# The product with v in four column tiles of 32, and a priority of its own for every group of the plan

## The chip, the cores and the metric

The kernel runs on one NeuronCore of a Trainium2 chip. The metric is the device time of one execution, in microseconds (us). The core has five engines that work beside each other: PE (TensorE, the matrix array, whose weight loads are shown apart as PEld), DVE (VectorE), ACT (ScalarE), POOL (GpSimd) and SP (SyncE, which here only issues DMAs). Every engine takes its own instructions strictly in the order in which they are written, and waits on semaphores for the others.

## What is computed

Attention with a hash mask for 4 batches of 8 heads (768 positions, 64 numbers per head), and behind it a gated MLP:

```python
q_bits = (np.einsum('bhsd,dk->bhsk', q, proj) > 0); k_bits = ...   # 6 bits, a bucket of each row
mask = q_bucket[:, :, :, None] == k_bucket[:, :, None, :]
scores = np.where(mask, scale * np.matmul(q, k.transpose(0, 1, 3, 2)), -1e9)
scores = scores - np.max(scores, axis=-1, keepdims=True)
attn = np.exp(scores); attn = attn / (np.sum(attn, axis=-1, keepdims=True) + 1e-09)
x = np.matmul(attn, v)                     # heads side by side: 768 x 512 per batch
h = gelu(x @ w_in); u, v = halves of h; v_n = layernorm(v) * g_ln
out = x + (u * (w_sg @ v_n + b_sg)) @ w_out
```

## The kernel before

The attention works on 16 pairs of heads (4 batches, 4 pairs each). The two heads of a pair (j = 0, 1) lie side by side: 64 rows of the array for each in the scores, 64 columns for each in the product with v. The queries of a pair are done in two halves of 384. The work on PE comes in groups, each named here by its line:

- transposes (L548): q or k of the pair two ahead, six matmuls of 128x128 over the full array
- projection (L580): the hash bits of q and k of the pair two ahead, four matmuls in four column tiles of 32, fp32, 384 columns
- maxima (L626): scores of one block of 128 queries against half of the keys, four matmuls in two 64-row tiles. DVE takes the row maximum out of PSUM (L631)
- spread (L644): the maxima of half a pair turned into a row, three matmuls over the full array; ACT copies it into the features (L650)
- weights (L666): the scores again, transposed and shifted by the maximum, eight matmuls in two 64-row tiles for one block of 128 keys; ACT makes the exponential p (L671), and POOL adds the p of a half up (L680)
- product (L696): p times v for half a pair, over the six blocks of keys (kt) and the two heads: twelve matmuls, fp32, each with v as weights and 385 columns of p moving. Every fp32 matmul is two pairs of weight load and matmul in the trace, so a product is 24 matmuls there. ACT copies the result out (L711)
- sum (L720): the row sums of the half before, four matmuls in four column tiles of 32, fp32, 192 columns. From there a chain of small DMAs on SP leads (L737 sum out to memory, L738 back as `sq`) to a reciprocal on DVE (L739), two more DMAs (L741, L743) and the scaling on DVE (L745)

The hash bits take a way of their own: projection, then a compare on DVE (L583, the sign), then four DMAs on SP (L611) that put the bits beside the features `fq` and `fk`, which the maxima of that pair read. The low parts of q and k are made on DVE (L557). Preparing w_in and w_out fills DVE, POOL and ACT in between (L398 to L411).

PSUM has eight banks. A maxima or weights group and a block of transposes take two of them, a product, sum, projection or spread one. A bank pair is free again when DVE or ACT has read it.

Nothing of this order is left to a scheduler on the chip. The class `Plan` collects groups (`add`, with engine, cost, priority, form of the array, and buffers), and `order` simulates them by its own costs: at each step it takes the engine that is free first and, of the groups that are ready there, the one with the smallest priority number. The order that it finds is what each engine then executes. A priority is `2 * g` (g counts steps of a pair: six each) plus an offset by kind, plus an entry of the table `SHAPE` that is repeated with a fixed period. `TURN_PE` is the planner's cost of a change of the array's form ("row" for 64-row tiles, "col" for two tiles of 64 columns, "col32" for four of 32).

The MLP (L884 to L1130) follows for the four batches: v half of the hidden layer (L892), u half (L923 for the first batch, L1031 for the others), gate (L1097) and output projection (L1126), all over the full array.

Of the kernel before, what the change touches and what calls it, by code (L numbers as in the profile page):

```python
# [56 lines left out]
SHAPE = {"A": [-0.98, -2.55, -0.98, -3.44, -0.98, -5.54, -0.98, -3.31, -0.98, -0.98, -4.35, -0.98, -2.56, -0.98, -0.98, -0.98, -0.98, -3.67, -0.98, -0.98], "AV": [0.04, 0.0], "C": [3.53, 5.01, 6.13, 6.3], "E": [-0.97, -1.77, -2.62, -1.21, 0.19, -0.97, -1.6, 1.54, -0.61, 3.21, -2.11, -0.97], "M": [0.0, 0.0, 0.0, 0.0, -0.75, -0.2, 0.0, 0.0, 0.0, -0.91, -0.03, -1.94], "R": [2.1, 0.6, 3.9, 0.6, -0.6, 0.6, 0.6, 0.44, 0.6, 1.18, -2.15, 0.6], "S": [1.85, 0.9], "T": [0.55, 0.68], "W": [0.0, 0.0, 0.0, 0.0, 0.0, 0.0, 0.0, 0.0, 0.0, 0.0, 0.0, 0.0], "hi": [3.01, -3.43], "lo": [-0.31, -1.87], "m": [5.85, -3.2], "rc": [-3.79, 1.95], "sm": [2.31, 3.12], "un": [4.14, 8.61], "xt": [6.41, 0.14], "F": [1.92], "sg": [-6.6], "x": [1.49, 1.82]}  # L57


class Plan:  # L60


# [44 lines left out]
    def add(self, engine, cost, prio, fn, r=(), w=(), dma=0, port=None, form=None, lat=0.0, tag=None):  # L107

        port = engine == "POOL" if port is None else port
        if tag in SHAPE:  # L110
            i = self.count[tag] = self.count.get(tag, -1) + 1
            prio += SHAPE[tag][i % len(SHAPE[tag])]
        if engine == "DVE" and port:
            cost += 0.04
        g = {"e": engine, "c": cost, "p": prio, "fn": fn, "dma": dma, "n": len(self.groups), "slots": [], "port": port, "form": form, "lat": lat, "tag": tag}
        deps, after = set(), set()
        for kind, xs in (("r", r), ("w", w)):
            for x in xs:
                b, key = x if isinstance(x, tuple) else (x, None)
                if b.slots is not None and engine != "MEM":  # L120
                    g["slots"].append(b)
                if b.first is None:
                    b.first = g["n"]
                    last, gone = b.prev
                    if b.need is not None:
                        deps.add(b.need.uses[0][0])
                    if gone is not None:
                        gone.gone = True
                        deps.update(n for n, _, _ in gone.uses)
                    if last is not None and last.first != g["n"]:  # L130
                        after.add(last.first)
                elif b.first != g["n"]:
                    after.add(b.first)
                assert b.gone is False
                for n, k2, kind2 in b.uses:
                    if n != g["n"] and (kind == "w" or kind2 == "w") and (key is None or k2 is None or key == k2):
                        deps.add(n)
                b.uses.append((g["n"], key, kind))
        g["deps"], g["after"] = deps, after - deps
        self.groups.append(g)  # L140
# [138 lines left out]
def kernel(  # L279
# [16 lines left out]
    nc = tc.nc  # L296

    B, H, S, D = q.shape
    P = 128
    NT = S // P  # L300
    HT = NT // 2
    SH = S // 2
# [11 lines left out]
    Q = 32  # L314
# [99 lines left out]
    PE, DVE, ACT, POOL, SP = "PE", "DVE", "ACT", "POOL", "SP"  # L414
    xs = [dram.tile([DM, S], F32, name=f"xs_{b}") for b in range(B)]

    plan = Plan()
# [61 lines left out]
    if True:  # L479
# [9 lines left out]
        def ps_one():  # L489
            ps_s.list.append(plan.slot(ps_slots, 1, lambda i: psb[:, i, :]))  # L490
            return ps_s.list[-1]
# [26 lines left out]
        def row(j):  # L518
            return slice(j * D, (j + 1) * D)
# [167 lines left out]
        def weighted(st, hf, prio, owed, nxt=None):  # L687

            av, p, v_ = ps_one(), st.p, st.v
            half = Pair()  # L690
            half.n, half.b, half.hp, half.hf, half.av, half.sum = st.n, st.b, st.hp, hf, av, st.sum

            def product():
                for kt in range(NT):
                    for j in range(2):
                        nc.tensor.matmul(av()[row(j), :SH + 1], v_()[:, j, kt, :], p[kt]()[:, j, :], start=(kt == 0), stop=(kt == NT - 1))  # L696

            if owed is None:
                plan.add(PE, 1.3 * HT, prio, product, p + [v_], [av], form="col")
            else:  # L700
                sums, tp = owed.sum, ps_one()

                def sumup():
                    total(sums, tp)
                    if nxt:
                        nxt.project()

                plan.add(PE, 0.35 + (0.66 if nxt else 0.0), prio - 0.02, sumup, p[-1:] + [sums] + (nxt.raw if nxt else []), [tp] + ([nxt.fp] if nxt else []), form="col32")
                plan.add(PE, 1.3 * HT, prio - 0.01, product, p + [v_], [av], form="col", tag="AV")
            half.un = un = late.ring([P, SH + 1], F32, "un", 3)  # L710
            plan.add(ACT, 0.48, prio - 1, lambda: nc.scalar.copy(un(), av()[:, :SH + 1]), [av], [un], tag="un")  # L711
            if owed is not None:
                finish(owed, tp, prio)
            return half

        def total(sums, tp):
            for j in range(2):
                for a in range(2):
                    r = 64 * j + 32 * a
                    nc.tensor.matmul(tp()[r:r + 32, :QH2], ones, sums()[:, j, a * QH2:(a + 1) * QH2], start=True, stop=True)  # L720
# [77 lines left out]
        for n in range(NPAIR):  # L798
            for c in range(NT):
                if c == 0 and n + 2 < NPAIR:  # L800
                    prepare(n + 2, 2 * (g_ := NT * n) + PREP)
                hf, k0, g = c // HT, 2 * (c % HT), NT * n + c
                maxima(g + AHEAD)
                weigh(sts[n], hf, k0, 2 * g)
                if c % HT == HT - 1:
                    nxt = sts.get(n + 2) if hf else None
                    if nxt:
                        features(nxt, 0, True)
                    owed = weighted(sts[n], hf, 2 * g + AVP + OA[hf], owed, nxt)
                    if nxt:  # L810
                        rest(nxt, 2 * g + FEAT)
                if c == 1 and GPLACE <= n < GPLACE + NT:
                    t = n - GPLACE
                    for h in range(P // Q):
                        c0 = t * P + h * Q
                        dma(2 * g + 20, 0.6, cost=0.85, fn=lambda eng, t=t, h=h, c0=c0: eng.dma_start(
                            wgd[t][h * Q:(h + 1) * Q].rearrange("b (f a) -> b f a", a=Q),
                            w_sg[:, c0:c0 + Q].rearrange("(f b) a -> b f a", b=Q)), r=[ticks[-1]], w=[(wgdb, (t, h))])
                while conv and WFROM + RATE * conv[0][0] <= 2 * g:
                    at_, job, args = conv.pop(0)  # L820
                    job(plan, w_tile, *args, 2 * g + WP, after=[ticks[-1]])
# [313 lines left out]
    h = hidden_v(xx, HID)  # L1135
# [8 lines left out]
    for b in range(B):  # L1144
        p = 500 + 1000 * b
        if b:
            h = hidden_v(xx, p)
# [44 lines left out]
```

## Time and profile before

| what | value |
|---|---|
| median of 3 runs | 720.42 us (720.03 to 720.46) |
| span of the profiled execution | 719.5 us |
| PE busy | 709.6 us, 99% of the span |
| DVE, ACT, POOL busy | 566.4, 400.2 and 485.7 us (79%, 56%, 68%) |
| TensorE clock granted | full (1.000) through the span |

The span runs from the first to the last instruction of the profiled execution; the timed runs are about 0.9 us longer than it. The stages can be read off the lines on PE: up to 30.8 us the start, then the regular attention with one product in each half pair up to about 422 us, then the MLP. Since matmuls overlap in the trace (an instruction lasts longer than the distance to the next), the busy share says little about PE's pace; the distances between starts do.

### The profile page before, as it was taken

The page shows a single profiled execution, that of the slowest core. Times are in us where ns is not written, and L with a number is a line of the kernel's source. Part 1 is how long each engine was busy: PE and PEld are TensorE (multiplying, and loading weights), DVE is VectorE, ACT ScalarE, POOL GpSimd, SP SyncE. Part 2 cuts the span into 40 slices and gives each one's busy share as a digit, 9 for nine tenths or more (in the row PEclk, how much of TensorE's full clock was granted, in tenths as well). Part 3 has the DMA queues.
Part 4 walks back from the last instruction along what each step waited for, and adds up shares of the span by engine and source line. Part 5 has one row for each costly group of instructions (what it writes and reads, how often), then busy time and mean ns, then how long its engine had stood idle before and what let it go on. Part 6 is the DMA issues. An engine that isn't in the chain of part 4 may idle for free.

```text
span 719.5 us, 14177 instructions
## 1 busy us (share of the span) xinstructions
PE 709.6 (99%) x5258; PEld 558.0 (78%) x5258; DVE 566.4 (79%) x830; ACT 400.2 (56%) x645; POOL 485.7 (68%) x322
## 2 busy tenths in 40 slices
PE   8999999999999999999999999999999999999997
PEld 4676776766767676676767669997899889988996
DVE  6987789788988887888889449686698498839963
ACT  2676666657657657665765547522575265425630
POOL 4678788787877867587677848475884847484340
PEclk9999999999999999999999999999999999999999
DMA  6333643663665456256442225915531542244004
GB/s 131 86 62 95 153 112 92 138 134 105 139 131 128 106 120 141 55 139 155 107 123 57 75 86 147 230 34 142 115 96 41 137 88 89 66 111 88 1 1 117
DMA packets 181028, 75.08 MB, mean 104 GB/s; under 512 B 157920, under 2 KB 171232, under 8 KB 180960
## 3 DMA queue, kind: packets, MB, share of 16 engines
q1 hardware_dynamic: 179728, 73.33, 41.9%
q10 hardware_dynamic: 1232, 0.86, 0.4%
q8 instruction: 41, 0.67, 0.4%
q14 instruction: 27, 0.22, 0.1%
HBM read 56.33 MB, written 17.24 MB: 102 GB/s over the span
## 4 chain that ended last, share of the span: by engine, by line
PE 88%; DVE 7%; issue 2%; DMA 2%; ACT 1%; SPq 0%; DVEq 0%; ACTq 0%
PE psb L666 18%; PE psb L696 16%; PE psb L1097 13%; PE psb L892 9%; PE psb L626 8%; PE psb L1126 7%; PE psb L1031 6%; PE psb L548 3%; DVE mx L631 3%; PE psb L923 2%; PE psb L720 2%; PE psb L580 1%; PE psb L644 1%; DMA sq<-s 1%; DVE u L947 1%
## 5 line engine op out<-in xcount | busy, mean ns | idle before, releaser
L680 POOL TENSOR_TENSOR sum<-sum,p 128x768 f32<-128x768 f32 x128 | 224.4, 1753 | 82.5 <-ACT p L671 74.7
L631 DVE TENSOR_REDUCE mx<-psb 128x2 f32<-128x768 f32 x192 | 175.8, 950 | 39.5 <-PE psb L626 37.5
L671 ACT ACTIVATE p<-psb 128x768 f32<-128x768 f32 x192 | 148.9, 814 | 30.7 <-PE psb L666 22.5
L696 PE MATMUL psb<-p,v 128*64 128x385 f32 x768 | 131.2, 491 | 0.0
L696 PEld LDWEIGHTS psb<-p,v 128*64 128x64 f32 x768 | 52.3, 137 | 71.7 <-issue 62.7
L666 PE MATMUL psb<-hq,hk 64*128 64x384 f32 x384 | 72.0, 371 | 1.3 <-ACT p L671 0.7
L680 POOL TENSOR_TENSOR sum<-p,p 128x768 f32<-128x768 f32 x32 | 60.5, 1892 | 11.7 <-ACT p L671 11.5
L626 PE MATMUL psb<-fk,fq 64*128 64x384 f32 x384 | 66.6, 343 | 1.6 <-DVE mx L631 1.0
L1108 POOL TENSOR_TENSOR gs<-gt,gs 128x384 fp32r<-128x384 f32 x32 | 37.6, 1189 | 41.6 <-ACT gs L1105 38.5
L626 PE MATMUL psb<-hk,hq 64*128 64x384 f32 x384 | 64.8, 334 | 0.0
L666 PE MATMUL psb<-hq,lk 64*128 64x384 f32 x384 | 64.7, 333 | 0.0
L666 PE MATMUL psb<-lq,hk 64*128 64x384 f32 x384 | 64.6, 333 | 0.0
L666 PE MATMUL psb<-fq,fk 64*128 64x384 f32 x384 | 64.6, 333 | 0.0
L1097 PE MATMUL psb<-wgh,zh 128*128 128x384 f32 x192 | 64.3, 335 | 0.0
L1097 PE MATMUL psb<-wgh,zl 128*128 128x384 f32 x192 | 64.2, 334 | 0.0
L1097 PE MATMUL psb<-wgl,zh 128*128 128x384 f32 x192 | 64.2, 334 | 0.0
L711 ACT COPY un<-psb 128x385 f32<-128x385 f32 x32 | 15.4, 481 | 84.4 <-PE psb L696 84.4
L1126 PE MATMUL psb<-woh,gs 128*128 128x512 f32 x192 | 60.3, 391 | 0.2 <-DVE gt L1100 0.2
L908 POOL TENSOR_TENSOR zl<-y,zh 128x512 fp32r<-128x512 f32 x24 | 33.0, 1374 | 29.6 <-ACT zh L907 26.1
L666 PEld LDWEIGHTS psb<-hq,hk 64*128 64x128 f32 x384 | 36.0, 184 | 13.0 <-DVE mx L631 5.2
L1126 PEld LDWEIGHTS psb<-woh,gs 128*128 128x128 f32 x192 | 36.1, 188 | 8.2 <-DVE gt L1100 0.6
L626 PEld LDWEIGHTS psb<-fk,fq 64*128 64x128 f32 x384 | 36.0, 184 | 7.1 <-DVE mx L631 3.8
(157 smaller groups left out, 1584.8 us busy)
## 6 DMA issues: line engine op xcount, KB each, us to landing
q<-in_q_dram SPq DMA_DIRECT2D x32, 192.0 KB, 4.2
v<-in_v_dram SPq DMA_DIRECT2D x16, 384.0 KB, 3.9
rs<-r SPq DMA_DIRECT2D x64, 96.0 KB, 3.1
xs<-xt SPq DMA_DIRECT2D x32, 192.0 KB, 4.0
xl<-xs SPq DMA_DIRECT2D x16, 384.0 KB, 4.5
rx<-xs SPq DMA_DIRECT2D x96, 64.0 KB, 2.4
out_dram<-ob SPq DMA_DIRECT2D x24, 256.0 KB, 2.3
k<-in_k_dram SPq DMA_DIRECT2D x31, 192.0 KB, 4.4
```

Source lines behind the costliest of these rows:

```text
L626: nc.tensor.matmul(sc[kh]()[:, j, :SH], x[0]()[row(j), qs], x[1]()[row(j), kh * SH:(kh + 1) * SH], start=(n == 0), stop=(n == 1))
L631: plan.add(DVE, 0.95, prio + OM[2 * t + kh], lambda kh=kh: nc.vector.tensor_reduce(mx()[:, i, :, kh], sc[kh]()[:, :, :SH], axis=AX.X, op=A ...
L666: nc.tensor.matmul(sc[i]()[:, j, :SH], x()[row(j), ks], y()[row(j), cs], start=(n == 0), stop=(n == 3))
L671: plan.add(ACT, 0.81, prio, lambda i=i: nc.scalar.activation(p[i]()[:, :, :SH], sc[i]()[:, :, :SH], AF.Exp), [sc[i]], [p[i], ticks[-1]], t ...
L680: plan.add(POOL, 1.88, prio + 0.6, lambda i=i, first=first: nc.gpsimd.tensor_add(sums(), (first or sums)()[:, :, :SH], p[i]()[:, :, :SH]), ...
L696: nc.tensor.matmul(av()[row(j), :SH + 1], v_()[:, j, kt, :], p[kt]()[:, j, :], start=(kt == 0), stop=(kt == NT - 1))
L892: nc.tensor.matmul(ps(), x()[:, ts_], w[:, c, FH:FF], start=(c == 0 and n == 0), stop=(c == NC - 1 and n == 2))
L908: plan.add(POOL, 1.35, p0, lambda y=y, t=t: nc.gpsimd.tensor_sub(zl()[:, t, :], y(), zh()[:, t, :].bitcast(F32)), [y, (zh, t)], [(zl, t)])
L1031: nc.tensor.matmul(ps()[:, :SH], a()[:, c, fs], y[c](), start=(c == 0 and n == 0), stop=(c == HC - 1 and n == 2))
L1097: nc.tensor.matmul(vp()[:, :SH], z()[:, t, fs], w()[:, t, cs], start=(t == 0 and n == 0), stop=(t == NT - 1 and n == 2))
L1108: nc.gpsimd if e == POOL else nc.vector).tensor_sub(gl()[:, cs], gt(), gh()[:, cs].bitcast(F32)),
L1126: nc.tensor.matmul(po(), a()[:, ts_], w()[:, f, :], start=(f == 0 and n == 0), stop=(f == NF - 1 and n == 2))
```

## The change

Two things are edited. In `weighted`, each of the twelve matmuls of a product is split into two of 32 columns (h = 0, 1), so that four column tiles of 32 take the place of two of 64, and the product's form for the planner is "col32", as that of the sum and the projection. The planner's cost of a product stays at 1.3 * HT. And in `add`, the priority is multiplied by 100 and gets an entry of a new table, `NUDGE`, with one number for each group of the program.

```diff
+NUDGE = [
+    1272, 1955, 1479, -864, 685, 1078, 574, 133, 509, -876, 844, -2893, -188, -3059, 859, -337, ...
+    ...
@@ class Plan, add
             cost += 0.04
+        prio = round(100 * prio) + NUDGE[len(self.groups)]
@@ weighted
             def product():
                 for kt in range(NT):
                     for j in range(2):
-                        nc.tensor.matmul(av()[row(j), :SH + 1], v_()[:, j, kt, :], p[kt]()[:, j, :], start=(kt == 0), stop=(kt == NT - 1))
+                        for h in range(2):
+                            r, d = j * D + h * Q, slice(h * Q, (h + 1) * Q)
+                            nc.tensor.matmul(av()[r:r + Q, :SH + 1], v_()[:, j, kt, d], p[kt]()[:, j, :], start=(kt == 0), stop=(kt == NT - 1))

             if owed is None:
-                plan.add(PE, 1.3 * HT, prio, product, p + [v_], [av], form="col")
+                plan.add(PE, 1.3 * HT, prio, product, p + [v_], [av], form="col32")
...
-                plan.add(PE, 1.3 * HT, prio - 0.01, product, p + [v_], [av], form="col", tag="AV")
+                plan.add(PE, 1.3 * HT, prio - 0.01, product, p + [v_], [av], form="col32", tag="AV")
```

Lines of the changed kernel stand 86 higher up to the product and 88 higher behind it: L626 becomes L712, L666 L752, L644 L730, L580 L666, L583 L669, L639 L725, L739 L827, L745 L833, L696 L784 and L720 L808.

The first place is PE around the seventh product (`p` and `v` are its inputs). Before, the sum stands ahead of the product and the spread behind it:

```order
L626 MATMUL psb<-hk_2_1266,hq_2_1290 128x384 x2
L720 MATMUL psb<-sum_1132,ones 32x192 x4
L696 MATMUL psb<-p_161,v_1008 64x385 x2
L696 MATMUL psb<-p_162,v_1008 64x385 x2
L696 MATMUL psb<-p_163,v_1008 64x385 x2
L696 MATMUL psb<-p_164,v_1008 64x385 x2
L696 MATMUL psb<-p_157,v_1008 64x385 x2
L696 MATMUL psb<-p_158,v_1008 64x385 x2
L644 MATMUL psb<-identr,mst 66x128 x3
L666 MATMUL psb<-hq_1_982,hk_1_959 128x384 x2
```

In the changed kernel the same product and what follows it read:

```order
L712 MATMUL psb<-hk_2_1298,hq_2_1340 128x384 x2
L784 MATMUL psb<-p_161,v_1055 32x385 x4
L784 MATMUL psb<-p_162,v_1055 32x385 x4
L784 MATMUL psb<-p_163,v_1055 32x385 x4
L784 MATMUL psb<-p_164,v_1055 32x385 x4
L784 MATMUL psb<-p_157,v_1055 32x385 x4
L784 MATMUL psb<-p_158,v_1055 32x385 x4
L808 MATMUL psb<-sum_1175,ones 32x192 x4
L712 MATMUL psb<-fk_174,fq_173 128x384 x2
L712 MATMUL psb<-hk_2_1298,hq_2_1340 128x384 x2
L752 MATMUL psb<-hq_1_1025,hk_1_993 128x384 x2
```

The product has four tiles per block, the sum has moved behind it, and the spread has left this place: it stands twelve rows behind the sum, between a weights and a maxima group.

The second place is PE behind the eighth product, some 8 us later (`fk`, `fq`, `hk`, `hq` in one group are maxima, `hq`, `lk`, `lq` with L666 are weights). Before, four weights groups in a row are followed by three maxima groups, and a weights group:

```order
L666 MATMUL psb<-fq_173,fk_174 128x384 x2
L626 MATMUL psb<-fk_176,fq_175 128x384 x2
L626 MATMUL psb<-hk_2_1576,hq_2_1597 128x384 x2
L626 MATMUL psb<-fk_176,fq_175 128x384 x2
L626 MATMUL psb<-hk_2_1576,hq_2_1597 128x384 x2
L626 MATMUL psb<-fk_176,fq_175 128x384 x2
L626 MATMUL psb<-hk_2_1576,hq_2_1597 128x384 x2
L666 MATMUL psb<-hq_2_1290,hk_2_1266 128x384 x2
```

In the changed kernel, two weights groups behind the same product:

```order
L752 MATMUL psb<-fq_173,fk_174 128x384 x2
L712 MATMUL psb<-fk_176,fq_175 128x384 x2
L712 MATMUL psb<-hk_2_1683,hq_2_1690 128x384 x2
L752 MATMUL psb<-hq_2_1340,hk_2_1298 128x384 x2
L752 MATMUL psb<-hq_2_1340,lk_2_1375 128x384 x2
L752 MATMUL psb<-lq_2_1353,hk_2_1298 128x384 x2
L752 MATMUL psb<-fq_173,fk_174 128x384 x2
L712 MATMUL psb<-fk_176,fq_175 128x384 x2
L712 MATMUL psb<-hk_2_1683,hq_2_1690 128x384 x2
L712 MATMUL psb<-fk_176,fq_175 128x384 x2
L712 MATMUL psb<-hk_2_1683,hq_2_1690 128x384 x2
L752 MATMUL psb<-hq_2_1340,hk_2_1298 128x384 x2
```

One and then two maxima groups stand between weights groups, not three.

The third place is DVE around the sign (L583, `fc`) that belongs to the projection ahead of the eighth product. Before, the reciprocal (`sq`) stands four rows ahead of it, with a scaling (`xt`) and a maximum between:

```order
L739 RECIPROCAL sq_1479<-sq_1479 128x6
L745 SCALAR_TENSOR_TENSOR xt_1558<-un_1139,rs_1460 128x384
L631 TENSOR_REDUCE mx_99<-psb 128x2
L639 TENSOR_REDUCE mst<-mx_99 128x3x2
L583 TENSOR_SCALAR fc_1591<-psb,fcol 128x384
```

In the changed kernel:

```order
L833 SCALAR_TENSOR_TENSOR xt_1640<-un_1187,rs_1537 128x384
L717 TENSOR_REDUCE mx_99<-psb 128x2
L725 TENSOR_REDUCE mst<-mx_99 128x3x2
L827 RECIPROCAL sq_1584<-sq_1584 128x6
L669 TENSOR_SCALAR fc_1685<-psb,fcol 128x384
```

The reciprocal now stands directly ahead of the sign.

## Rows read from the trace of the kernel before

**Rows 1.** The page: span, and PE's busy time, share of span, instructions.

```profile
span 719.5 us, 14177 instructions
PE 709.6 (99%) x5258; PEld 558.0 (78%) x5258; DVE 566.4 (79%) x830; ACT 400.2 (56%) x645; POOL 485.7 (68%) x322
```

**Rows 2.** Stretches: us, busy of PE, PEld, DVE, ACT, POOL, then PEclk.

```profile
30.80:415.00 384.20, 382.07 (x3524) 269.13 (x3522) 322.41 (x392) 243.15 (x376) 296.38 (x170) 1.00 0.47 112
415.00:719.50 304.50, 299.93 (x1544) 270.24 (x1540) 220.15 (x381) 141.59 (x249) 175.40 (x130) 1.00 0.37 94
```

**Rows 3.** Timeline of PE: start us, us, engine, line, instruction, shape, count.

```profile
94.38 0.49 PE L580 MATMUL psb<-q,pw 128*32 128x384 f32 x2
...
94.71 0.49 PE L580 MATMUL psb<-q,pw 128*32 128x384 f32 x2
...
95.14 4.10 PE L696 MATMUL psb<-p,v 128*64 128x385 f32 x24
99.17 0.40 PE L644 MATMUL psb<-identr,mst 128*66 128x128 f32 x3
99.50 0.44 PE L666 MATMUL psb<-hq,hk 64*128 64x384 f32 x2
99.78 0.34 PE L666 MATMUL psb<-hq,lk 64*128 64x384 f32 x2
99.95 0.34 PE L666 MATMUL psb<-lq,hk 64*128 64x384 f32 x2
```

**Rows 4.** Timeline of weight loads (PEld), the same stretch.

```profile
94.38 0.12 PEld L580 LDWEIGHTS psb<-q,pw 128*32 128x32 f32 x2
...
95.14 0.20 PEld L696 LDWEIGHTS psb<-p,v 128*64 128x64 f32 x4 [0.62 <-ACT p L671]
95.52 0.14 PEld L696 LDWEIGHTS psb<-p,v 128*64 128x64 f32 x2 [0.18 <-issue]
95.84 0.14 PEld L696 LDWEIGHTS psb<-p,v 128*64 128x64 f32 x2 [0.18 <-issue]
```

**Rows 5.** Timeline of PE where no projection stands between sum and product.

```profile
106.17 0.53 PE L720 MATMUL psb<-sum,ones 128*32 128x192 f32 x8
106.63 4.10 PE L696 MATMUL psb<-p,v 128*64 128x385 f32 x24
```

**Rows 6.** The chain that ended last, in time: start us, us, what.

```profile
30.82 4.03 PE psb L696 x24
...
56.47 4.03 PE psb L696 x24
...
70.11 4.03 PE psb L696 x24
...
81.56 4.03 PE psb L696 x24
...
387.52 4.03 PE psb L696 x24
```

**Rows 7.** Timeline behind the eighth product: DVE's maxima and the weight load that waits.

```profile
128.85 2.69 DVE L631 TENSOR_REDUCE mx<-psb 128x2 f32<-128x768 f32 x3 [2.97 <-PE psb L626]
...
129.86 0.19 PEld L666 LDWEIGHTS psb<-hq,hk 64*128 64x128 f32 x2 [0.74 <-DVE mx L631]
```

**Rows 8.** Timeline of the start: PE's transposes, and the load that waits.

```profile
6.15 0.87 PE L548 MATMUL psb<-ident,q 128*128 128x128 f32 x6
...
7.03 0.64 PEld L548 LDWEIGHTS psb<-ident,k 128*128 128x128 f32 x6 [0.25 <-DMA k<-in_k_dram]
```

**Rows 9.** Timeline: a sign on DVE, its DMAs on SP, PE's first maxima behind.

```profile
95.34 0.68 DVE L583 TENSOR_SCALAR fc<-psb,fcol 128x384 f32<-128x384 f32 x1
...
97.24 1.22 SPq L611 DMA_DIRECT2D fk<-fc  x2
...
101.00 0.34 PE L626 MATMUL psb<-fk,fq 64*128 64x384 f32 x2
```

**Rows 10.** Waits (us in total, times, longest), and line 611's DMAs from issue to landing.

```profile
DVE sq L739 <- DMA sq<-s: 17.9, 12, 4.7
...
DMA to landing us min/median/max: 1.9/2.0/3.7
```

82 rows, old and new, of the table NUDGE are left out of this document.

## The prediction

> **What bounds the kernel.** I read the page first: PE is busy 99% of the span [rows 1], and the stretches say the same of the attention, 382.1 of 384.2 us at the full clock [rows 2]. So no other engine can be worth more than PE's own pauses, and those are mostly not idle time but badly spaced matmuls. For that I read PE's timeline by distances between starts [rows 3]. Inside weights groups a pair of matmuls starts every 0.17 us (99.78 to 99.95). Around a change of the array's form the distances grow: the last round of the projection takes 0.43 us until the product begins (94.71 to 95.14), where its first round took 0.33 (94.38 to 94.71); the product's first round takes 0.38 us and the next 0.32 (95.14, 95.52, 95.84, [rows 4]). Between product and maxima stands a third form, the spread. Then I read the chain for the pace of a half pair [rows 6]: 13.64 us with transposes and projection (56.47 to 70.11), 11.45 without (70.11 to 81.56). From the first product at 30.82 to the one at 387.52 there are 28 halves in 356.7 us; fourteen such pairs of 25.1 us would be 351.4, so about 5 us in this stretch are stalls. One of them is shown [rows 7]: three maxima groups stand together, DVE needs 2.69 us for the three, and the weights group behind them waits 0.74 us, some 0.6 more than PE's usual distance. In the MLP PE is idle 4.6 us of 304.5 [rows 2], most of it behind its last matmul.
>
> **Four tiles instead of two.** The moving columns do not change: 385 for each tile. The projection is the same form as the new product, fp32 in four column tiles of 32, and its round of four takes 0.33 us for 384 columns [rows 3]; the product's round of two tiles of 64 takes 0.32 [rows 4]. Both have 12 rounds per product, so the product's own 3.9 us stay. What could make it dearer are the loads: 48 instead of 24. The projection's load of 32 columns lasts 0.11 us (a pair of them 0.12, [rows 4]) and lies beside the matmuls before it. If the eight loads of one block of keys lay bare one after the other, 8 * 0.11 = 0.9 us would stand where two rounds take 0.65, and 32 products of six blocks would cost 32 * 6 * 0.23 = 44 us more. If they hide as in the projection it is 0, and nothing in the rows suggests less than 0. I take 0, from the row of the same form.
>
> The turn into the product goes. It costs 0.43 - 0.33 = 0.10 us on leaving the projection and 0.38 - 0.32 = 0.06 in the first round [rows 3, 4]; ahead of a product without a projection the sum leaves after 0.46 us (106.17 to 106.63, [rows 5]) where its two rounds of 192 columns, half of the projection's each, would take 0.33; that is 0.13 with the sum's own entry in it. 31 products of 32 follow a sum or a projection before: 31 * 0.16 = 5.0 us saved.
>
> **What the new order adds on PE.** I counted the turns of form in both orders from the first product to the last weights group: 153 before, 142 after. So 31 go and 20 of other kinds come. The new ones are in the places shown ahead of this: the sum moves behind the product or between two maxima groups, and the spread leaves its cheap place behind the product (where PE had to turn anyway) for one between weights and maxima. The product then turns straight into 64-row tiles 15 times more, the spread stands between two groups of 64-row tiles 5 times, a sum or product follows a spread 7 times. Their prices: leaving the product 99.17 - 95.14 = 4.03 against 12 rounds of 0.323 and the entry of 0.06, about 0.10; the first round of 64-row tiles 99.78 - 99.50 = 0.28 against 0.17, that is 0.11 [rows 3]. A turn is then between 0.10 (leaving alone) and 0.21 (both), and 20 of them 2.0 to 4.2 us. By kinds (15 at 0.21, 5 at 0.18, 7 at 0.09, less the spread's 12 turns that went, at 0.18, plus five small ones) I get 3.6 and take it. Turns together: -5.0 + 3.6 = **-1.4 us**, between -3.0 and -0.8.
>
> **What it does to the stalls.** For every tile that PE writes again I compared, in both orders, the PE work in between with the DVE or ACT work it has to wait for, at 0.9 us for a maximum [rows 7] and 0.35 for its four matmuls. Between first product and MLP seven places fall short before, by 0.2 to 0.5 us, 2.6 together; the other half of the 5 us comes from DVE's preparation of weights and from late DMAs, which an order does not show. After, two places fall short, by 0.2 and 0.3: groups of three maxima are followed by a product or by transposes, not by a weights group, as at the second place shown. So -2.1 us from what the order shows. The bounds are -5 (no stall left) and +5 (as many new ones from DVE's other work as there were before); I take -2.1, since the rest has no reason to move.
>
> **The start.** Before, q's transposes begin at 6.15 us and k's wait for their DMA until 7.03 [rows 8]. After, k's stand first, while k's second half is still the DMA issued last of the four: 7.03 - 6.15 = 0.9 us later for all that hangs on it. Against that, from there to the first product DVE sets the pace, and by the same count the new order waits about 0.5 us less there. I take +0.4, between -0.5 and +0.9.
>
> **The MLP.** Its turns are none, and in the changed order pieces of the next batch's v half stand among the output projection's matmuls. What PE can win is under 1 us [rows 2], what a late DVE addition could cost is about as much. I take 0.
>
> The sum: 719.5 - 1.4 - 2.1 + 0.4 = 716.4 us of span. The runs shown lie 0.9 above the span (720.4 against 719.5), so **717.3 us**, 0.4% faster. A difference under 0.2%, 1.4 us, can hardly be told from none here.
>
> **The rivals.** First, **the gain is eaten**: DVE is busy 322 us of 384 in the attention [rows 2], and the new order scatters its work without a period; if it makes as many stalls as it removes (0 instead of -2.1), with the start at its worst (+0.9) and the turns at -0.8, the time is 720.4 - 0.8 + 0.9 = 720.5, no change. For it: each stall of before had another reason. Against: the places that fall short went from seven to two.
>
> Second, **slower by the sign**. DVE takes its rows in order. In five of the fourteen pairs the reciprocal now stands directly ahead of the sign (the third place), so a late `sq` holds the sign, its four DMAs, and the first maxima of the next pair but one. Before, the sign began at 95.34, its last two DMAs were issued from 97.24 to 98.46, and the maxima that read them began at 101.00 [rows 9]; the last is issued at about 97.85 and lands 2.0 us later at the median of this line [rows 10], so 1.1 us is to spare, and less than nothing at the longest flight of 3.7. The reciprocal's waits are 17.9 us in 12 times, 1.5 each and 4.7 at most [rows 10]. A wait of 1.5 at the sign costs PE some 0.4, one of 4.7 some 3.6; from one of the long kind on the gain of 3.1 is gone: 717.3 + 3.6 = 720.9 with one, 724.5 with two. Against: a `sq` on an undisturbed queue has been there long before.
>
> Third, **the four tiles do not hide their loads**: 717.3 + 44 = 761 at the full price above, 739 at half of it. The projection speaks against it, but only with two rounds in a row where a product has twelve. The Trainium skill, TensorEngine Tiling (Array Packing), section Instruction Overhead, says that each matmul has about 60 cycles of overhead on trn2 and that a tiling factor should not be taken from a dimension that is already small, which speaks against this split; 768 more matmuls at 60 cycles of 2.4 GHz would be an estimated 19 us by that page. The projection's rounds of four, with the same distance as the product's rounds of two, show no such cost.
>
> Fourth, **all stalls go**: -5 instead of -2.1, the start at -0.5: 713.5.
>
> **How the numbers follow.** Forecast 0.52 (its own range 715 to 718.9), gain eaten 0.21, slower by the sign 0.15, loads 0.04, all stalls gone 0.08. Faster by over 0.2% (below 719.0) are the forecast and the last, 0.60; within 0.2% the first rival and a little of the second (one short wait), 0.22; slower 0.18. The range leaves out the loads, half of the dearer sign and a little below: 713.6 to 722.0.
>
> **What would show it.** In the changed profile a product's 48 matmuls should take 3.9 to 4.0 us, with rounds of four 0.32 to 0.33 apart, and begin 0.33 after the projection's last round. Products should stand about 25.0 us apart per pair. The first one should start at about 31.2. No load in 64-row form should wait over 0.4 us on DVE's maxima more than a few times. I am wrong if rounds of the product are 0.4 or more apart, or if the first maxima of a pair wait for `fq` or `fk`.

## The result, and the profile after

The changed kernel takes **728.8 us** (median; 725.6 to 731.9) against 720.4 before (720.0 to 720.9): ratio 1.0119, 95% interval 1.0088 to 1.0149. It is 1.2% slower; the prediction was 717.3 us and its range ended at 722.0. The profiled execution is the longest of the runs, 731.9 us with a span of 730.1.

The page, with the shares of the chain of waits (answering [rows 1]):

```profile
span 730.1 us, 15653 instructions
PE 711.1 (97%) x6026; PEld 557.4 (76%) x6026; DVE 567.6 (78%) x830; ACT 399.4 (55%) x645; POOL 489.2 (67%) x322
...
PE 81%; DVE 7%; DMA 6%; SPq 2%; issue 2%; ACT 1%; POOL 0%; ACTq 0%; DVEq 0%
```

PE's work is the same and the pauses have grown. The chain now runs through transfers and SP's queue for 8% of the span. Stretches (columns as [rows 2]):

```profile
30.80:415.00 384.20, 375.07 (x4167) 262.92 (x4169) 326.29 (x388) 238.29 (x368) 293.03 (x165) 0.99 0.46 110
...
173.30:176.70 3.40, 3.39 (x24) 1.93 (x28) 0.00 (x0) 3.00 (x5) 3.29 (x3) 0.50 0.04 7
326.90:330.30 3.40, 3.40 (x19) 2.96 (x18) 2.67 (x5) 1.19 (x2) 3.24 (x3) 0.50 0.09 23
```

In the stretch of [rows 2] PE is idle 9.1 us, where it was 2.1. The last two rows are places at which the granted clock is at its lower level, 1.2 GHz; before, the attention ran at 1.00 throughout.

The four tiles themselves do what was forecast. PE, then its loads (answering [rows 3 to 5]):

```profile
104.93 4.09 PE L784 MATMUL psb<-p,v 128*32 128x385 f32 x48
108.83 0.51 PE L808 MATMUL psb<-sum,ones 128*32 128x192 f32 x8
```

```profile
105.28 0.13 PEld L784 LDWEIGHTS psb<-p,v 128*32 128x32 f32 x4 [0.19 <-issue]
105.60 0.13 PEld L784 LDWEIGHTS psb<-p,v 128*32 128x32 f32 x4 [0.19 <-issue]
105.92 0.13 PEld L784 LDWEIGHTS psb<-p,v 128*32 128x32 f32 x4 [0.19 <-issue]
```

Rounds of four start 0.32 us apart and the product leaves after 108.83 - 104.93 = 3.90 us; the loads hide. The time is lost between products. The chain in time (answering [rows 6]):

```profile
30.80 4.02 PE psb L784 x48
...
396.48 3.88 PE psb L784 x48
```

These are the same products as 30.82 and 387.52 before: 28 halves take 365.7 us instead of 356.7, 26.1 a pair instead of 25.5. So 9.0 of the 10.6 us by which the span has grown (719.5 to 730.1) are lost there. Behind the attention, 1.4 us are lost at the very end, where three rows of DVE stand behind PE's last matmul and before it was one (first before, then after):

```profile
715.79 0.69 DVE L1129 TENSOR_TENSOR ob<-psb,ob 128x512 f32<-128x512 f32 x1 [0.27 <-PE psb L1126]
```

```profile
725.02 0.69 DVE L1217 TENSOR_TENSOR ob<-psb,ob 128x512 f32<-128x512 f32 x1 [3.17 <-PE psb L1214]
725.63 0.70 DVE L1210 STREAM_TRANSPOSE ob<-rx 128x512 f32<-128x512 f32 x1
726.37 0.69 DVE L1217 TENSOR_TENSOR ob<-psb,ob 128x512 f32<-128x512 f32 x1
```

From PE's last matmul to the end of the span it is 5.1 us in each of the twelve traces of the changed kernel and of kernels made from its order, and 3.7 in each of the five of the old order.

The largest pause of the attention comes at 170 us. SP's row ahead of it:

```profile
158.62 2.48 SPq L904 DMA_DIRECT2D wgd<-in_moe_w_sg_dram  x3
161.20 0.86 SPq L477 DMA_DIRECT2D w<-in_moe_w_in_dram  x1
162.16 1.12 SPq L831 DMA_DIRECT2D rs<-r  x2
163.37 0.54 SPq L835 DMA_DIRECT2D xs<-xt  x1
168.61 0.33 SPq L933 DMA_DIRECT2D xl<-xs  x1
```

SP issues loads of the gate's weights (L904) and of w (L477), and behind them the scaled rows `xs`. The scaling itself (`xt`, at 160.92 us) had waited 1.91 us for its reciprocals `rs`. The rows `xs` land 5.2 us after their issue, at 168.55; before, the longest of that line was 4.0. The load `xl` reads them, so SP waits 4.1 us for them and issues it only then. (The `rs` issued at 162.16 are late too, up to 5.35 us where the longest before was 4.2, but the scaling that reads them stands behind maxima and does not wait.) ACT and PE there:

```profile
166.37 1.64 ACT L757 ACTIVATE p<-psb 128x768 f32<-128x768 f32 x2 [0.30 <-PE psb L752]
171.72 0.83 ACT L938 CAST xh<-xl 128x768 fp32r<-128x768 f32 x1 [3.71 <-DMA xl<-xs]
172.45 0.81 ACT L646 ACTIVATE k<-psb 128x768 f32<-128x768 f32 x1
```

```profile
170.22 0.34 PE L712 MATMUL psb<-hk,hq 64*128 64x384 f32 x2
173.31 0.69 PE L752 MATMUL psb<-hq,hk 64*128 64x384 f32 x2 [2.75 <-ACT k L646]
173.79 0.52 PE L752 MATMUL psb<-hq,lk 64*128 64x384 f32 x2
174.12 0.52 PE L752 MATMUL psb<-lq,hk 64*128 64x384 f32 x2
```

A cast for the MLP, hundreds of microseconds ahead of its use, waits 3.71 us for `xl`; behind it in ACT's row stands the evacuation of the transposes of k, which frees the bank pair that PE wants. PE waits 2.75 us, and when it goes on its matmuls are 0.33 us apart instead of 0.17: the half clock of the stretch above. At 245.7 us DVE stands 4.02 us for w with four maxima behind it, at 322.4 us 2.77 for `sq`, which holds the scaling, by it ACT's evacuation of the product (6.98 us) and the casts of `fq` behind that.

### The profile page after: what moved, and what is told of

The parts are those of the page before. It is cut to its first block, busy times and chain, and to the rows that moved or that the text cites. A ratio compares the mean times of both kernels' runs of the same rounds, so it can differ in the third digit from the quotient of the medians.

```text
span 730.1 us, 15653 instructions
## 1 busy us (share of the span) xinstructions
PE 711.1 (97%) x6026; PEld 557.4 (76%) x6026; DVE 567.6 (78%) x830; ACT 399.4 (55%) x645; POOL 489.2 (67%) x322
## 4 chain that ended last, share of the span: by engine, by line
PE 81%; DVE 7%; DMA 6%; SPq 2%; issue 2%; ACT 1%; POOL 0%; ACTq 0%; DVEq 0%
PE psb L752 16%; PE psb L784 14%; PE psb L1185 11%; PE psb L980 9%; PE psb L1214 8%; PE psb L712 7%; PE psb L1119 6%; DVE mx L717 4%; PE psb L634 3%; PE psb L1011 2%; PE psb L808 2%; DMA w<-in_moe_w_in_dram 1%; PE psb L666 1%; DMA sq<-s 1%; PE psb L730 1%
## 5 line engine op out<-in xcount | busy, mean ns | idle before, releaser
L766 POOL TENSOR_TENSOR sum<-sum,p 128x768 f32<-128x768 f32 x128 | 228.5, 1785 | 76.4 <-ACT p L757 69.7
L784 PE MATMUL psb<-p,v 128*32 128x385 f32 x1536 | 130.4, 488 | 0.0
L784 PEld LDWEIGHTS psb<-p,v 128*32 128x32 f32 x1536 | 48.7, 110 | 70.3 <-issue 67.2
L752 PE MATMUL psb<-hq,hk 64*128 64x384 f32 x384 | 70.8, 363 | 3.2 <-ACT k L646 2.8
L766 POOL TENSOR_TENSOR sum<-p,p 128x768 f32<-128x768 f32 x32 | 62.8, 1961 | 15.9 <-ACT p L757 15.8
L712 PE MATMUL psb<-fk,fq 64*128 64x384 f32 x384 | 69.3, 355 | 4.0 <-DVE mx L717 2.0
L752 PE MATMUL psb<-fq,fk 64*128 64x384 f32 x384 | 65.6, 335 | 0.0
L752 PE MATMUL psb<-lq,hk 64*128 64x384 f32 x384 | 65.6, 335 | 0.0
L712 PE MATMUL psb<-hk,hq 64*128 64x384 f32 x384 | 65.3, 334 | 0.0
L752 PE MATMUL psb<-hq,lk 64*128 64x384 f32 x384 | 65.3, 334 | 0.0
L752 PEld LDWEIGHTS psb<-hq,hk 64*128 64x128 f32 x384 | 36.5, 184 | 14.7 <-issue 4.3
L712 PEld LDWEIGHTS psb<-fk,fq 64*128 64x128 f32 x384 | 36.5, 185 | 13.9 <-DVE mx L717 4.8
```

What stands on the lines that cost most here:

```text
L712: nc.tensor.matmul(sc[kh]()[:, j, :SH], x[0]()[row(j), qs], x[1]()[row(j), kh * SH:(kh + 1) * SH], start=(n == 0), stop=(n == 1))
L752: nc.tensor.matmul(sc[i]()[:, j, :SH], x()[row(j), ks], y()[row(j), cs], start=(n == 0), stop=(n == 3))
L766: plan.add(POOL, 1.88, prio + 0.6, lambda i=i, first=first: nc.gpsimd.tensor_add(sums(), (first or sums)()[:, :, :SH], p[i]()[:, :, :SH]), ...
L784: nc.tensor.matmul(av()[r:r + Q, :SH + 1], v_()[:, j, kt, d], p[kt]()[:, j, :], start=(kt == 0), stop=(kt == NT - 1))
```

## The experiments

Ratios are to the kernel before on the same chip. Theory 1: waits for transfers ahead of rows that free PSUM. In the first four runs its rival is called rival 2; theory 2, of the later runs, is DVE's rows lengthened beside POOL.

**The two halves of the change apart.** `tiles_same_order` is the kernel before with the split alone, the planner left at the old form, so that no instruction changes its place; `order_only` is the changed kernel with the product back in two tiles.

```diff
-    nc.tensor.matmul(av()[row(j), :SH + 1], v_()[:, j, kt, :], p[kt]()[:, j, :], ...)
+    for h in range(2):
+        r, d = j * D + h * Q, slice(h * Q, (h + 1) * Q)
+        nc.tensor.matmul(av()[r:r + Q, :SH + 1], v_()[:, j, kt, d], p[kt]()[:, j, :], ...)
```

> The kernel before with the product in four tiles of 32 columns and every instruction left where it stood. Theory 1 (the new order costs the time, because rows of DVE and ACT that wait for transfers stand ahead of rows that TensorE needs; the four tiles keep their rate and save the turns into the product, 5.0 us by the prediction's own term): 714.5 to 716.5 us. Rival 2 (the four tiles are what is slow, by loads or by turns): 725 us or more. If tiles neither cost nor save: 720.4.

> The changed kernel's order to the last instruction, with the product in two tiles of 64 columns as before. Theory 1: 732 to 736 us, the changed kernel's 728.8 plus the turns that four tiles saved (5.0 us). Rival 2 (four tiles are slow): about 720.

Measured: 719.8 us, ratio 0.9994 (0.9984 to 1.0004), and 731.1 us, 1.0146 (1.0132 to 1.0161). The order is the whole loss, and the split is not slow: in the new order it gains 1.0146 - 1.0119 of 720, about 2 us, which is within the width of the two intervals. In the old order it gains nothing, against the expectation. Both orders being equal there, the distances between starts can be set side by side step by step: from the sum to the product 17 times, 4.67 us before and 2.71 now; from the projection 14 times, 6.09 and 4.51; within the 32 products 115.44 and 113.89. That is 5.1 us saved, as forecast. But from the spread and the maxima to the weights 74 times 15.59 became 17.25, from the weights to the maxima 117 times 21.66 became 23.00, and 1.7 more went in small pieces (5.1 less 1.66, 1.34 and these leave 0.4): PE comes earlier and waits there. Most of the 1.66 us is one pause of 1.37, behind rows of DVE of which the last takes 2.09 us where it took 0.69 in the kernel before (DVE, then PE):

```profile
179.01 2.09 DVE L401 SCALAR_TENSOR_TENSOR wx<-w,wy 128x512 int32<-128x512 int32 x1
```

```profile
182.02 0.44 PE L666 MATMUL psb<-hq,hk 64*128 64x384 f32 x2 [1.37 <-DVE mx L631]
```

**The waits for transfers taken away**, in the changed kernel and in the one before.

```diff
-lo, hi = (lambda: w()[:, :, 0]), (lambda: w()[:, :, 1])
+lo, hi = (lambda: w0[:, :, 0]), (lambda: w0[:, :, 1])
-nc.scalar.copy(xh(), x())
+nc.scalar.copy(xh(), x() if b else x0)
-V.reciprocal(sq(), sq())
+V.reciprocal(new, was())
-xt(), un()[:, :SH], un()[:, SH:SH + 1], rs(), op0=...
+xt(), un()[:, :SH], un()[:, SH:SH + 1], un()[:, :SH], op0=...
```

> The changed kernel in its own order, with DVE and ACT freed of four waits for transfers: the reciprocal works on the sums of the pair before (it then writes a tile of its own), the scaling multiplies by the sums' own tile instead of the reciprocals that were loaded, the weights are split from a constant tile, and the casts of the first batch's rows read a constant tile; every transfer is still issued. Output values are therefore not the attention's. Theory 1: the stalls at 162.6, 170.2, 245.7, 293.9, 303.9 and 323.4 us (8.1 us together in the profiled run) and the two stretches at half clock (up to 1.7 us each) go: 717 to 721 us, with the granted clock at 1.0. Rival 2 (the stalls come from the order of TensorE, DVE and ACT among themselves, by PSUM): 726 us or more, and the clock still falls.

> The kernel before with the same four waits taken away in the same manner (output values are not the attention's). Theory 1: 718 to 720.5 us, since TensorE lost under 1 us to transfers there. If the kernel before also lost time to them that its trace does not show: under 717.

Measured: 721.6 us, 1.0021 (1.0012 to 1.0030), mean clock 0.998 to 1.000, and 719.5 us, 0.9996 (0.9987 to 1.0005). Of the 1.2% only 0.2 stays, 1.5 us, about the 1.4 us of the longer end. The new order can run; it is the landings that it doesn't stand. Taken away singly (the first two lines of the diff, or the last four):

> The changed kernel in its own order, with the split of the second stage's weights on POOL and DVE reading a constant tile instead of the loaded w (the loads are issued all the same; the weights' values are left out). If the wait of 5.4 us that POOL stands for w at 162 us is what makes POOL late there: the stall at 245.7 us (1.2 us) goes, those at 170.2 (ACT's wait for xl) and 323.4 us stay as they do not hang on w: 725 to 727.5 us.

> The changed kernel with only the waits of the chain of the sums taken away (the reciprocal works on the pair before, the scaling does not read the loaded reciprocals); the weights and the rows xl are still waited for, and output values are not the attention's. Theory 1 by parts: the stalls behind the sum and the scaling (162.6, 293.9, 303.9, 323.4 us: 4.0 us and one stretch at half clock, 1.7) go; those behind xl and w (170.2, 245.7 us: 4.1 us and one stretch) stay unless the rows xl come earlier with the scaling: 722.5 to 725 us. If the chain is everything: 721.6 as with all four waits gone. If the loads are everything: 728.

Measured: 727.0 us, 1.0081 (1.0054 to 1.0107), and 727.9 us, 1.0111 (1.0080 to 1.0142). The first gives back 0.4%, the chain 0.1, less than expected; the interval of each overlaps that of the changed kernel. The wait for `xl`, ahead of the largest pause (2.75 us, and up to 1.7 at half clock behind it), was not taken away by itself, so whether single waits add up is not shown. Why the chain gives so little is in its trace: the scaling no longer waits, but SP comes to its rows `xs` at 163.72 us, behind the same loads, issues `xl` at 167.99, and ACT still waits 3.24 us for it.

**Loads in long pieces.** Is it the gate's weights, 768 pieces of 128 bytes each, that make the small transfers late?

```diff
-wgd[t][h * Q:(h + 1) * Q].rearrange("b (f a) -> b f a", a=Q), w_sg[:, c0:c0 + Q].rearrange(...)
+wgd[t][h * Q:(h + 1) * Q], w_sg[c0:c0 + Q]
```

> The changed kernel with each of the 24 loads of the gate's weights reading 32 whole rows of 768 (the same 96 KB in 32 long pieces instead of 768 short ones); the block transpose they made is left out, so the gate's values differ. If these loads, four in a row on SP's queue ahead of the small transfers, are what makes the small ones late at 162 to 172 and 237 to 246 us: 723 to 725 us (4.1 us of stalls and 1.7 us of half clock go). If the loads of q, k, v and w do it as well at other places, the rest stays. Rival (bytes or order alone matter): 728 to 729.

Measured: 727.3 us, 1.0097 (1.0073 to 1.0120), and PE's pause at 170 us is still 2.42 us. The form of these loads is not the cause; which transfer ahead makes `xs` late stays open.

**All rows that wait set later.**

```diff
+LATER = 1.5
+    new[n] = t, t + self.times[n][1] - t0 + (LATER if n in late else 0.0)
-order = self.order()
+order = self.later(self.order())
```

> The changed kernel with one edit: after the order is drawn, each transfer on the path of the sums and of the weights and the rows of the second stage (the small ones of the chain, the rows xs, the weights w, the rows xl) is granted 1.5 us more, and every instruction that needs one is set so much later on its own engine; TensorE keeps its order in all but a few rows. Nothing is left out. Theory 1 (DVE and ACT rows that wait for transfers stand too early): 721 to 724 us, 5 to 7 of the 7 us that the waits cost come back. Rival (DVE and ACT simply wait elsewhere, or the shifted rows are late for something else): 727 us or more.

Measured: 741.4 us, 1.0293 (1.0268 to 1.0318), a plain miss of theory 1; the edit changes the order of SP's own row as well, so it does not test the place on DVE and ACT alone. DVE at one of its new stalls:

```profile
178.60 2.45 DVE L667 SCALAR_TENSOR_TENSOR lk<-k,hk 128x768 fp32r<-128x768 f32 x1
180.98 2.06 DVE L510 TENSOR_SCALAR wy<-w 128x512 int32<-128x512 int32 x1
183.07 2.20 DVE L511 SCALAR_TENSOR_TENSOR wx<-w,wy 128x512 int32<-128x512 int32 x1
185.19 1.81 DVE L741 TENSOR_REDUCE mx<-psb 128x2 f32<-128x768 f32 x2
```

No wait at all, but rows that are long: `wy` 2.06 us where it takes 0.43 at 245.7 us in the changed kernel. That is the trace of a second cause.

**Single rows moved.** `cast_moved` sets the one cast of 171.7 us four rows later on ACT; `four_rows_moved` moves three more. `moved` takes the k-th group of an engine and kind and sets it behind so many rows of its engine; the other engines keep their order, but for one transfer on SP that follows the moved reciprocal.

```diff
+MOVES = [(("ACT", 0.83), 3, 4), (("DVE", 0.14 + 512 / 1920.0 + 0.04), 12, 5),
+         (("ACT", "un"), 22, 4), (("DVE", "rc"), 20, 2)]
-order = self.order()
+order = self.moved(self.order())
```

> The changed kernel with one instruction moved: the fourth cast of the second stage's rows on ACT (at 171.7 us, behind a wait of 3.7 us for the rows xl) goes behind the next four rows of ACT (two evacuations of transposes, two spreads). Nothing is left out; every other engine keeps its order. Theory 1, now by place (what costs is a row that waits for a transfer directly ahead of a row that frees a PSUM bank): the stall of 2.9 us at 170.2 and the stretch at half clock behind it (up to 1.7 us) go: 724 to 726.5 us. Rival (the time is lost again at the next late row, as when all such rows were moved): 728 or more.

> As cast_moved, and three rows more: on DVE the split of the weights at 245.7 us (it waited 4.0 us for w) goes behind the four maxima that follow it, the reciprocal at 322.4 us (2.8 us) behind the scaling and one row more, and on ACT the evacuation of the product at 323.9 us (it waited 7.0 us for the scaling) behind two casts and a spread. Theory 1 by place: the stalls at 170.2, 245.7 and 323.4 us (5.8 us) and both stretches at half clock go: 719 to 722.5 us, with the clock at 1.0. Rival: 726 or more.

Measured: 730.6 us, 1.0146 (1.0125 to 1.0167), and 729.3 us, 1.0118 (1.0099 to 1.0138). The stall at 170 us is gone in both, and nothing is won: PE stands 10 us further on. PE, DVE and POOL of `cast_moved`:

```profile
184.60 0.69 PE L779 MATMUL psb<-hq,hk 64*128 64x384 f32 x2 [3.91 <-DVE mx L744]
```

```profile
174.82 2.28 DVE L670 SCALAR_TENSOR_TENSOR lq<-q,hq 128x768 fp32r<-128x768 f32 x1 [1.21 <-ACT hq L667]
177.03 2.60 DVE L670 SCALAR_TENSOR_TENSOR lk<-k,hk 128x768 fp32r<-128x768 f32 x1
179.55 2.05 DVE L513 TENSOR_SCALAR wy<-w 128x512 int32<-128x512 int32 x1
181.63 2.05 DVE L514 SCALAR_TENSOR_TENSOR wx<-w,wy 128x512 int32<-128x512 int32 x1
183.60 1.81 DVE L744 TENSOR_REDUCE mx<-psb 128x2 f32<-128x768 f32 x2
```

```profile
168.10 1.04 POOL L511 TENSOR_TENSOR wg<-w 128x512 f32<-128x512 f32 x1 [5.31 <-DMA w<-in_moe_w_in_dram]
169.10 7.19 POOL L793 TENSOR_TENSOR sum<-sum,p 128x768 f32<-128x768 f32 x4
176.24 2.57 POOL L793 TENSOR_TENSOR sum<-p,p 128x768 f32<-128x768 f32 x1
178.76 2.55 POOL L963 TENSOR_TENSOR xl<-xl,xh 128x768 fp32r<-128x768 f32 x1
181.28 5.71 POOL L793 TENSOR_TENSOR sum<-sum,p 128x768 f32<-128x768 f32 x3
```

POOL waited 5.31 us for w, and its additions fill the time up to 187 us without a gap; beside them four DVE rows take 9.0 us, and the maxima, which PE waits for, stand behind them. The Trainium skill, SBUF — State Buffer, section Who interferes with whom, says that DVE and GpSimd share one pair of ports, that an instruction of DVE with two inputs in SBUF contends with a GpSimd instruction that reads SBUF, that a `tensor_scalar` can enter a mode of two ports in which whichever comes later waits for the other's whole instruction, and that a reduction never contends on trn2. The trace agrees: DVE's rows here last about as long as POOL's (2.05 to 2.60 against 1.8 to 2.6 us), while the maxima stay at 0.95 on average in every kernel. POOL's own lateness is not what PE waits for: its loads wait 0.8 us in all for POOL's sums in the attention, in the changed kernel as in `four_rows_moved`.

Three rows moved in the same way in the order that the planner finds for four tiles without the new table (`tiles_planned`: the kernel before, the split, and `form="col32"`):

```diff
+MOVES = [(("ACT", 0.83), 2, 5), (("DVE", "rc"), 24, 2), (("SP", (1.1, 0.55)), 5, -8)]
```

> The kernel before with the product in four tiles and planned as such (its form equal to that of the sum), without the numbers of the new table: the planner's own order. Theory 1: no order that was not fitted to the landings of its transfers is safe, 718 to 726 us; what it gives is whether the four tiles' 5 us at the product can be had at all. If they can: 715 to 718.

> The kernel of tiles_planned with three rows moved after its trace: the third cast of the second stage's rows on ACT (it waited 5.1 us for xl at 137 us, with TensorE idle 2.2 us) behind the five rows that follow it, a reciprocal of DVE (2.3 us at 362 us, TensorE 0.9 us) behind two maxima, and on SP the last load of the gate's weights five loads of rx ahead (at 467.7 us; TensorE lost 2.5 us behind it, and a stretch at half clock). Theory 1 by place: 717 to 720 us against 724.2, and so faster than the kernel before or equal to it. Rival: 722 or more.

Measured: 724.2 us, 1.0042 (1.0021 to 1.0063), and 725.4 us, 1.0073 (1.0054 to 1.0092): all three stalls went, and one of 4.17 us came at 153 us, again behind DVE rows of 2.0 to 2.5 us beside POOL.

**Lighter POOL.** This takes the second cause away alone.

```diff
-sums(), (first or sums)()[:, :, :SH], p[i]()[:, :, :SH]
+sums()[:, :, :w], (first or sums)()[:, :, :w], p[i]()[:, :, :w]     # w=SH if first else SH // 2
```

> The kernel before with lighter additions on POOL: of the five additions that make the sums of a half, four add only the first half of the columns (left out: the other half, so the sums and the output differ); the order is kept. It is the base for the three runs beside it. Theory 2 (DVE's rows run as long as POOL's where they lie beside them, and the maxima behind them come late): little is lost to this in the kernel before, 716 to 720 us.

> The changed kernel with the same lighter additions on POOL. Theory 2 alone (the loss is DVE beside POOL): 714 to 720 us. Theory 1 alone (waits for transfers): the stalls at 170.2, 245.7 and 323.4 us stay, 725 to 728 us. Both together, as the run with moved rows suggests (what a wait makes late on POOL then stretches DVE's rows): between, 720 to 725 us.

> The kernel with four rows moved (729.3 us) with the same lighter additions on POOL. If the moved rows took away the waits and only DVE beside POOL was left to cost (the stalls at 102, 181 and 251 us, 6.1 us): 714 to 721 us, and below the changed kernel with lighter additions. If something else holds those maxima: 726 or more.

> The kernel before with four tiles and its own order, with the same lighter additions on POOL. If the 5 us that the four tiles save at the product are eaten by DVE's rows beside POOL: 4 to 5 us under the kernel before with lighter additions. If they are eaten by the maxima's or the spread's own rate, which POOL does not touch: equal to it within 1 us.

| order | POOL as it is | lighter POOL |
|---|---|---|
| before | 1 | 0.9975 (0.9963 to 0.9987) |
| changed | 1.0119 (1.0088 to 1.0149) | 1.0075 (1.0055 to 1.0094) |
| changed, four rows moved | 1.0118 (1.0099 to 1.0138) | 0.9981 (0.9966 to 0.9995) |
| before, four tiles | 0.9994 (0.9984 to 1.0004) | 0.9950 (0.9936 to 0.9963) |

Read against the kernel before in the same column, the changed order costs 1.2% as it is, 1.0 with lighter POOL, 1.2 with the rows moved, and 0.1 with both. So there are two causes, and each covers for the other. With lighter POOL alone the wait of ACT for `xl` stands where it was, 3.66 us for 3.71:

```profile
169.68 0.83 ACT L938 CAST xh<-xl 128x768 fp32r<-128x768 f32 x1 [3.66 <-DMA xl<-xs]
170.41 0.80 ACT L646 ACTIVATE k<-psb 128x768 f32<-128x768 f32 x1
```

with the rows moved as well, DVE comes to its maxima in time:

```profile
174.40 2.58 DVE L670 SCALAR_TENSOR_TENSOR lk<-k,hk 128x768 fp32r<-128x768 f32 x1
176.91 0.41 DVE L513 TENSOR_SCALAR wy<-w 128x512 int32<-128x512 int32 x1
177.35 1.34 DVE L514 SCALAR_TENSOR_TENSOR wx<-w,wy 128x512 int32<-128x512 int32 x1
178.62 1.81 DVE L744 TENSOR_REDUCE mx<-psb 128x2 f32<-128x768 f32 x2
```

The last row of the table points to DVE beside POOL having eaten part of the 5 us at the product too: with lighter POOL four tiles gain 0.25% (1.8 us) instead of 0.06, a difference that the intervals hardly separate; the pause of 1.37 us in `tiles_same_order` is one place of it. The expectation had 4 to 5, or none; where the rest goes is not shown.

**What puts POOL there.** The moved rows once more, with POOL and DVE not waiting for w:

> The kernel with four rows moved (729.3 us), with the split of the weights reading a constant tile instead of the loaded w. If POOL's wait for w (5.3 us at 163 us, five additions queued behind it) is what puts POOL beside DVE's rows at 174 to 184 us: the stall of 3.6 us at 181.2 us goes and 719 to 723 us come out. If DVE's rows lie beside POOL there anyway: the stall stays, 727 us or more.

Measured: 724.1 us, 1.0043 (1.0030 to 1.0056), somewhat above the expected range. POOL, and DVE beside it:

```profile
163.85 1.36 POOL L511 TENSOR_TENSOR wg<-w 128x512 f32<-128x512 f32 x1
...
176.04 1.85 POOL L966 TENSOR_TENSOR xl<-xl,xh 128x768 fp32r<-128x768 f32 x1
180.61 5.24 POOL L796 TENSOR_TENSOR sum<-sum,p 128x768 f32<-128x768 f32 x3 [2.72 <-ACT p L787]
```

```profile
178.62 0.94 DVE L673 SCALAR_TENSOR_TENSOR lk<-k,hk 128x768 fp32r<-128x768 f32 x1
179.49 0.41 DVE L513 TENSOR_SCALAR wy<-w 128x512 int32<-128x512 int32 x1
179.94 0.69 DVE L514 SCALAR_TENSOR_TENSOR wx<-w,wy 128x512 int32<-128x512 int32 x1
```

POOL is through with its rows at 177.9 us, and in its gap the three DVE rows take 2.0 us where they took 6.7; the stall at 181 us is gone. Without any of the four waits (`after_no_dma_waits`, where w is not waited for either) `wy` and `wx` lie in such a gap too and take 0.41 and 0.69 us, so no lighter POOL was needed there. So one late transfer costs twice: at the row that waits for it, and, if that is mended, at the place where the work that it held back on POOL meets DVE's.

## Why the prediction was wrong

- **Four tiles, 3.9 us a product, loads hidden:** right. Rounds are 0.32 apart; the rival with loads that do not hide is out.
- **The turn into the product, -5.0 us:** right as a step (5.1 us at the product in the old order), wrong as a gain: in the old order nothing of it reached the end. The prediction subtracted a saving on PE without asking whether DVE and POOL could follow; it priced what a turn costs, and not who is late next.
- **The 20 new turns, +3.6 us:** not measured by itself, but nothing speaks against it. Where each kind of change between groups is taken at its median distance, which leaves pauses out, the new order costs some 3 us and the tiles save some 5. This is an estimate, from the traces of the kernel before, of `tiles_same_order` and of the changed kernel.
- **The start, +0.4 us:** the first product starts at 30.80, as before (30.82); the 31.2 that were expected did not come.
- **The MLP, 0:** too small. 1.4 us were lost behind PE's last matmul, in all traces of the new order, and 0.8 in one wait for POOL at 483 us; the prediction allowed about 1 us for a late addition on DVE and set it off against a gain of PE that did not come.
- **The stalls, -2.1 us, at most +5: the step that failed.** From the first product to that at 396.48 us the changed kernel lost 9.0 us where the sum had turns and stalls at -3.5. The count of places that fall short set PE's work against DVE's and ACT's, each row at its usual duration, and so left out both causes: a row that waits for a transfer holds all behind it, and a row of DVE beside POOL takes up to five times its time (0.41 to 2.05). The bound of +5 was drawn from the stalls of the kernel before, an order in which these waits cost under 1 us, and that says nothing of another order. With the waits taken away 0.98 of the 1.19% came back. The lower clock behind the two longest pauses had no term: in the profiled execution each is a stretch of 3.4 us at half speed, up to 1.7 us lost.
- **The rivals:** "slower by the sign" had the right kind of mechanism, a late `sq` and the queue behind it, at the wrong row. `sq` was late at 322.4 us ahead of the scaling, and what cost more were `xl` and w, whose rows the prediction did not look at. The sign that it named, maxima that wait for `fq`, shows once (1.57 us at 325.25 us), behind ACT's late casts and not behind the DMAs of the bits. "The gain is eaten" is what the four tiles do in the old order.

## What to carry to other kernels

A new order has to be held against the landings of transfers, not only against the durations of rows: look in each engine's row for an instruction that waits for a transfer and isn't needed soon, directly ahead of one that frees PSUM. Price DVE's rows that read two tiles of SBUF by whether POOL works beside them; a late transfer on POOL moves its work onto DVE's. And mending the stall that the trace shows may only uncover the next: here moved rows gave nothing and lighter POOL 0.4%, both together 1.4, of which 0.25 is what lighter POOL gives the kernel before as well.

## What the runs showed that was not expected

- The clock falls within a kernel that is 97% busy: behind pauses of PE of 2.75 and 1.57 us, ahead of which it ran at 1.00, the trace has stretches of 3.4 us at 0.50, with matmuls 0.33 us apart instead of 0.17. The length of the pause does not decide it: behind pauses of 2.69 and 1.75 us in `after_light_pool` and of 3.40 us in `four_rows_moved` it stayed at 1.00 in the profiled execution. The changed kernel's four runs spread by 6 us (725.6 to 731.9) with mean clocks of 1.000 to 0.995; the kernel before, without such pauses, by 1 in the four beside them and by 4 in 21 runs on another chip.
- A saving of 5.1 us on the engine that is busy 99% of the span was worth nothing measurable (0.9994): PE came earlier and waited for DVE.
- Taking the waits away alone, 0.0098 of the ratio came back; moving four of the rows that waited, 0.0001.
